# First layers of a fused attention and two-MLP kernel: conversions dealt out evenly, softmax sums on VectorE, transposes later, separate buffers for sums

## The chip, the cores and the metric

The kernel runs on one NeuronCore of a Trainium2 chip. The metric is the device time of one execution in microseconds (us). Engines are named as in the profile: PE is TensorE (matmul), PEld its weight load, DVE VectorE, ACT ScalarE, POOL GpSimd and SP SyncE, which here only issues DMAs.

## The reference

Three steps follow one another, all in float32.

Attention: q, k, v have 4 batches, 8 heads, 768 positions and 64 features. The positions are cut into chunks of 32. A chunk sees 8 memory keys, 16 positions to its left, its own 32 and 8 to its right, 64 keys in all (fewer at the ends). Scores are scaled by 1/8, a softmax (maximum taken away, exponentials, division by their sum plus 1e-9) weighs v.

```python
x = attn_out.transpose(0, 2, 1, 3).reshape(3072, 512)
h = ((x @ w1) * (x @ w2)) @ w3 @ w_out            # w1, w2: 512x1024; w3: 1024x1024; w_out: 1024x512
y = ((h @ w_a) * (h @ w_b)) @ w_out2              # w_a, w_b: 512x1536; w_out2: 1536x512
```

## The kernel before, in words

**Precision.** Every matmul operand of the layers is split into a high part, rounded to the fp32r type by an ACT copy, and a low part, the difference. A product is then three matmuls (`PASSES`: high by high, high by low, low by high). Weights arrive as pairs of 32-bit words. A weight block is rebuilt from them by two scalings on ACT (`w_scale`, L381 and L382) and two operations on DVE (`w_bits`, L386 and L387), and then split.

**Stages.** (1) w3 @ w_out is multiplied out once (`wps`), beside the first attention units. (2) The first layers for token tiles 0 and 1 (512 tokens each) in plain form: for each of 8 column groups a product with w1 (`psA`) and one with w2 (`psB`), the product of both, and then y = g @ (w3 w_out) (`psY`, L816). (3) The first layers for tiles 2 and 3 (t = 2) and 4 and 5 (t = 4) in pair form: `seven12` computes one column group for two tiles as seven products of six matmuls each (Winograd's form of Strassen's scheme), a *pair step* of 42 matmuls. A half of four pair steps is followed by a y pass of 8 groups of 12 matmuls; there are two halves (h = 0 and 1) for each t. The second y pass adds to what the first stored in DRAM. Beside it, `x_build` makes the seven operands x of the next two tiles: it loads eight pieces from DRAM, forms differences (`minus`) and splits each result (`x_put`: high part on ACT, low part on DVE or POOL). (4) The second layers, also with seven products a step (`seven`), with an output product (`ops`).

**Attention** goes in 16 units of 192 tokens. A unit's stages are put into numbered slots: unit u starts at slot BASE[u], 7 slots after the unit before it from the sixth on. Scores (`sc`, in PSUM) come in slot 0, maximum and exponentials in slots 1 and 2 (`a_max`, 16 calls on ACT at L204, each with its sum), normalisation by POOL in slots 2 and 3 (`a_norm`, L221), transposes (`a_trans`, L232) and their copy (`a_pt`, L238) in slot 5, the products with v (`a_pv`, `xp`) in slot 6, the copy out (`a_x`) in slot 7 for units from the sixth on. `paced` spreads the slots over the steps of the layers, so that tile i has its input in time (`NEED`, `GOAL`). PE runs what is issued in that order.

**Conversion of w_a and w_b** (`c_weights`, generator `cw`): 12 blocks, each turned into seven pieces that are written to DRAM (`wcd`). A block is 12 steps: four rebuild its two halves, eight form sums (`add`, L519), split them (high part L102 on ACT, low part L105 on DVE, tile `co`) and issue the writes on SP. One step is taken at a time: in the plain form where nothing else is left to convert (`between`), and at three places in the pair form (`hook`): two in a pair step, one in each group of a y pass. What is left after t = 4 is issued in one loop (L977) before the second layers.

The weights of each pair step are loaded ahead by DMAs on POOL's queue (`w7_load`, L784). Low parts of g are formed on POOL in `g_split` (L876). A PSUM accumulator that gets further products is read between them: by ACT (`copied`, L862) or by DVE (`onto`, L866); PE cannot go on in that bank before.

Of the kernel before, what the change touches and what calls it, by code (L numbers as in the profile page):

```python
# [13 lines left out]
P = 128  # L14
# [11 lines left out]
ND = 2  # L26
# [20 lines left out]
def tile_attention_moe(  # L47
# [135 lines left out]
    def a_max(u):  # L183
# [12 lines left out]
        nc.vector.tensor_scalar_mul(mx, mx, -SCALE)  # L196
        soft[u] = (sc, t, mx, sm)

    def a_exp(i):
        def stage_of(u):  # L200
            sc, t, mx, sm = soft[u]
            for a in range(2 * i, 2 * i + 2):
                for r in range(2):
                    nc.scalar.activation(  # L204
                        t[:, a, r, :],
                        sc[:, r, a, :],
                        AF.Exp,
                        bias=mx[:, r, a : a + 1],
                        scale=SCALE,
                        accum_out=sm[:, a, r : r + 1],  # L210
                    )

        return stage_of

    def a_norm(e):
        def stage_of(u):
            t, mx, sm = soft[u][1:]
            t, sm = t[:, 4 * e : 4 * e + 4], sm[:, 4 * e : 4 * e + 4]
            nc.vector.tensor_scalar_add(sm, sm, 1e-9)
            nc.vector.reciprocal(sm, sm)  # L220
            nc.gpsimd.tensor_tensor(  # L221
                t, t, sm[:, :, :, None].to_broadcast([GQ, 4, 2, KEYS]), ALU.mult
            )

        return stage_of
# [33 lines left out]
    def a_x(u):  # L259
# [7 lines left out]
        for c0, c1 in zip(cuts, cuts[1:]):  # L267
            ti = c0 // TT
            src = xp[..., c0 - t0 : c1 - t0]
            if ti >= ND:  # L270
                xo = att.tile([P, KD, n], F32, tag="xo", bufs=1, name="xo")[:, :, : c1 - c0]
# [21 lines left out]
    for u in range(NA):  # L293
        t0, t1, t2, t3 = SLOTS.get(u, (6, 7, 8, 9) if u < NX else (5, 5, 6, 7))
        for s, stage_of in (
# [12 lines left out]
            (2 * (u > 0), a_exp(2)),  # L308
            (2 * (u > 0), a_exp(3)),
# [6 lines left out]
    for i in range(NT1):  # L316
        u = -(-TT * (i + 1) // (NE * GQ)) - 1
        NEED.append(BASE[u] + (8 if u >= NX else 10))
# [170 lines left out]
    def c_weights():  # L489
# [3 lines left out]
        def halves(items):  # L493
# [55 lines left out]
    co_in = [(stage, 2)]  # L549
# [96 lines left out]
    def d_weights():  # L646
        for m in range(M1):
# [17 lines left out]
            for i, p, q, op in (  # L665
# [11 lines left out]
                co = stage.tile([P, 2, CH // 2], F32R, tag="co", bufs=2, name="wo7")  # L677
# [15 lines left out]
    GOAL = [NEED[0], NEED[1] + 6, NEED[2 * ND - 1], NEED[-1]]  # L693
# [5 lines left out]
    def between():  # L699
# [35 lines left out]
    def x_tmp():  # L735
        if tps:
            return tps[-1].tile([P, TT], F32, tag="tmp", bufs=12 - 4 * len(tps), name="xb")
        ntmp[1] = (ntmp[1] + 1) % 4
        return tq[ntmp[1]]
# [5 lines left out]
    def x_build(xs, src, t, eng):  # L745
        for k in range(2):
            b11, b21, b12, b22 = (
                y_load(x_tmp(), src, t + j, i + k) for j in range(2) for i in (0, 2)
            )

            def minus(z, x, y):
                nc.vector.tensor_tensor(z, x, y, ALU.subtract)  # L752

            yield
# [5 lines left out]
            x_put(xs[3], k, b11, eng)  # L760
            minus(b12, b22, b12)
            yield
            x_put(xs[4], k, b12, eng)
            minus(b11, b22, b11)
            yield
            x_put(xs[2], k, b11, nc.vector)
            minus(b21, b21, b11)
            yield
            x_put(xs[5], k, b22, eng)
            yield  # L770
            x_put(xs[6], k, b21, eng)
            yield

# [16 lines left out]
    for ti in range(ND):  # L790
        last = ti == ND - 1
        gs = {}
        for m in range(M1):
            gs[m] = g_new(m)
            ab_step(w12s[m], xt[ti], gs[m], between)
            if last:
# [8 lines left out]
                else:  # L805
                    tq = wpool.tile([P, 4, CH], F32, tag="w12", name="tq")
                    tq = [tq[:, i, :] for i in range(4)]
# [71 lines left out]
    def seven12(w, ga, gb, hook):  # L879
# [3 lines left out]
        g_split()  # L883
        product(pb, 1, w, True)
        onto(c11, pb, c11, ALU.add)
        hook(1)
# [6 lines left out]
        hook(4)  # L893
        product(pc, 5, w, False)
        onto(c12, pc, c12, ALU.add)
        hook(5)
# [299 lines left out]
```

## Time and profile before

| | |
|---|---|
| median of 3 runs | 1248.08 us (1241.35 to 1250.42) |
| the profiled execution, its own time | 1247.78 us |
| its span, first to last instruction | 1246.0 us |
| mean granted PE clock | 0.929 of full speed |
| busy share of the span: PE, PEld, DVE, ACT, POOL | 87%, 69%, 43%, 39%, 25% |
| mean DMA traffic | 189 GB/s |

Busy shares are means over stages that differ. The page's slices show PE at nine tenths and more in the last 17 of 40 slices, and at 0 to 9 tenths with a granted clock between 0.5 and 1 in the slices before. A row is read by its stage: which engine PE waits for there, and what that engine had in front.

### The profile page before, as it was taken

The numbers are of one execution on the slowest core, as the hardware profiler recorded it, in microseconds if no ns is written. First come the engines' busy times: TensorE is split into PE (matmuls) and PEld (weight loads), VectorE is DVE, ScalarE is ACT, GpSimd is POOL, SyncE is SP. The second block draws the span as 40 slices with busy tenths as digits, with TensorE's granted clock in tenths as the row PEclk, the third lists the DMA queues.
The fourth block names the chain that finished last, engine by engine and source line by source line (L and its number), as shares of the span: only waits on it lengthen the run. The fifth ranks groups of instructions, "written<-read, shape, count | busy, mean of one in ns | idle before, by whom it ended". The sixth has DMA issues, their size and how long they took to land. (4 is left out here: it accounts for less than half of the span.)

```text
span 1246.0 us, 18964 instructions
## 1 busy us (share of the span) xinstructions
PE 1082.4 (87%) x7346; PEld 855.1 (69%) x7346; DVE 536.7 (43%) x870; ACT 481.0 (39%) x1231; POOL 314.3 (25%) x316
## 2 busy tenths in 40 slices
PE   9999886787788895799940499999999999999998
PEld 4457765575567674688730388888888888888887
DVE  6667644424552334554476643435323234232220
ACT  6768533543444442333234533333222223222220
POOL 0103424422331141332230123231133230232310
PEclk9999987888799998799975699999999999999999
DMA  9865588655468476465768656454243434434310
GB/s 372 254 189 174 153 254 270 208 153 175 177 204 264 160 246 201 171 252 195 251 202 286 243 201 221 172 195 160 93 178 125 171 135 144 152 130 167 143 69 34
DMA packets 99546, 234.99 MB, mean 189 GB/s; under 512 B 10240, under 2 KB 43392, under 8 KB 91520
## 3 DMA queue, kind: packets, MB, share of 16 engines
q1 hardware_dynamic: 84272, 138.31, 33.9%
q0 software_dynamic: 14976, 95.43, 20.7%
q8 instruction: 58, 0.95, 0.3%
q14 instruction: 32, 0.26, 0.1%
q10 hardware_dynamic: 208, 0.04, 0.0%
HBM read 176.07 MB, written 57.67 MB: 188 GB/s over the span
## 5 line engine op out<-in xcount | busy, mean ns | idle before, releaser
L850 PE MATMUL ps<-x,w 128*128 128x512 f32 x2184 | 525.3, 400 | 101.1 <-ACT tmp L862 75.1
L850 PEld LDWEIGHTS ps<-x,w 128*128 128x128 f32 x2184 | 420.5, 193 | 197.2 <-ACT tmp L862 78.1
L1014 DVE TENSOR_TENSOR tmp<-ps,tmp 128x512 f32<-128x512 f32 x108 | 74.6, 691 | 266.4 <-PE ps L850 236.2
L862 ACT ACTIVATE tmp<-ps 128x512 f32<-128x512 f32 x143 | 85.6, 599 | 215.9 <-PE ps L850 193.0
L93 PE MATMUL psY<-g,wo 128*128 128x512 f32 x576 | 143.1, 408 | 10.7 <-DVE tmp L866 10.7
L784 POOL DMA_DIRECT2D w<-wc x72 | 39.7, 553 | 416.4 <-PE ps L850 415.9
L93 PEld LDWEIGHTS psY<-g,wo 128*128 128x128 f32 x576 | 112.4, 197 | 36.8 <-DVE tmp L866 12.4
L93 PE MATMUL ops<-wo,g 128*128 128x512 f32 x504 | 118.6, 389 | 0.0
L93 PEld LDWEIGHTS ops<-wo,g 128*128 128x128 f32 x504 | 94.6, 188 | 19.6
L1020 ACT ACTIVATE g<-tmp 128x512 fp32r<-128x512 f32 x66 | 40.8, 633 | 139.4 <-DVE tmp L1019 139.4
L1021 POOL TENSOR_TENSOR g<-tmp,g 128x512 fp32r<-128x512 f32 x66 | 84.2, 1297 | 20.2 <-ACT g L1020 19.4
L204 ACT ACTIVATE t<-sc,mx 96x64 f32<-96x64 f32 x256 | 75.4, 318 | 35.8 <-DVE mx L196 35.8
L221 POOL TENSOR_TENSOR t<-t,sm 96x512 f32<-96x512 f32 x32 | 39.4, 1232 | 146.0 <-DVE sm L220 130.4
L102 ACT ACTIVATE x<-xb 128x512 fp32r<-128x512 f32 x56 | 34.2, 627 | 93.8 <-DVE xb L752 40.9
L93 PE MATMUL ops<-fo,g 128*128 128x512 f32 x288 | 68.2, 389 | 0.0
L93 PEld LDWEIGHTS ops<-fo,g 128*128 128x128 f32 x288 | 54.1, 188 | 11.2
L93 PE MATMUL wps<-w_f 128*128 128x512 f32 x128 | 60.3, 625 | 0.0
L866 DVE TENSOR_TENSOR tmp<-ps,tmp 128x512 f32<-128x512 f32 x47 | 32.4, 690 | 63.7 <-PE ps L850 51.2
L204 ACT ACTIVATION_READ_ACCUMULATOR t<-sc,mx 96x1 f32 x256 | 54.5, 213 | 0.0
L381 ACT ACTIVATE raw<-raw 128x512 f32<-128x512 f32 (+1 forms) x66 | 49.2, 745 | 12.8 <-DMA raw<-in_w3a 8.1
L93 PE MATMUL psA<-xt,w 128*128 128x512 f32 x192 | 51.5, 417 | 1.9 <-DVE w L417 1.8
L93 PE MATMUL psB<-xt,w 128*128 128x512 f32 x192 | 51.7, 422 | 0.0
(87 smaller groups left out, 1100.1 us busy)
## 6 DMA issues: line engine op xcount, KB each, us to landing
w<-wc POOLq DMA_DIRECT2D x36, 1024.0 KB, 6.6
w<-wc POOLq DMA_DIRECT2D x36, 768.0 KB, 4.7
wc<-co SPq DMA_DIRECT2D x84, 256.0 KB
w<-wd POOLq DMA_DIRECT2D x16, 1024.0 KB, 7.6
w<-wd POOLq DMA_DIRECT2D x16, 768.0 KB, 4.7
raw<-in_wab SPq DMA_DIRECT2D x24, 512.0 KB
v<-in_vw SPq DMA_DIRECT2D x64, 168.0 KB
kraw<-in_kt SPq DMA_DIRECT2D x16, 512.0 KB
```

The costliest lines, as they stand in the source:

```text
L93: nc.tensor.matmul(o, lhsT=l, rhs=r, start=first, stop=last)
L102: nc.scalar.activation(hi, src, AF.Copy)
L204: nc.scalar.activation(t[:, a, r, :], sc[:, r, a, :], AF.Exp, bias=mx[:, r, a : a + 1], scale=SCALE, accum_out=sm[:, a, r : r + 1],)
L221: nc.gpsimd.tensor_tensor(t, t, sm[:, :, :, None].to_broadcast([GQ, 4, 2, KEYS]), ALU.mult)
L381: nc.scalar.activation(h, h, AF.Prelu, scale=2.0**-112, alpha=2.0**32)
L784: nc.gpsimd.dma_start(out=t[:, c0:c1].bitcast(F32), in_=src[:, c0:c1])
L850: nc.tensor.matmul(ps, lhsT=w[:, i, a, k, :], rhs=xs[i][:, b, k, :], start=first and n == 0, stop=n == 5, skip_group_check=not first,)
L862: nc.scalar.activation(z, ps, AF.Copy)
L866: nc.vector.tensor_tensor(z, x, y, op)
L1014: nc.vector.tensor_tensor(z, ps, y, ALU.add)
L1020: nc.scalar.activation(g2[:, 0, :], z, AF.Copy)
L1021: nc.gpsimd.tensor_tensor(g2[:, 1, :], z, g2[:, 0, :].bitcast(F32), ALU.subtract)
```

## The change

1. Conversion: `between` takes no step of `cw` any more. `hook(attn, conv)` counts conversion places and takes steps so that 145 steps are spread over 78 of them; there are three in a pair step and one in each group of a y pass. The low parts of `co` move from DVE to POOL; `co` has four buffers from the start instead of two, and the extra pool `cop` is dropped.
2. Softmax: DVE subtracts the maximum from the scores (two operations, PSUM to SBUF), ACT takes two exponentials in place, DVE sums them (two reductions) in `a_norm`. Before, ACT took 16 exponentials with a bias and a sum each.
3. Slots: transposes, their copy, PV and copy out go from slots 5, 5, 6, 7 (for units 3 to 5 from 6, 7, 8, 9) to 8, 8, 9, 10; `NEED` and `GOAL` follow. `paced` in the pair form counts 40 hooks instead of 24. `xo` shares the buffer of `p2`.
4. `g_split` in a pair step comes after product 4 instead of product 0.
5. `x_build`: the differences get tiles of their own, loads are issued three and five steps ahead of their use, work is spread over more steps, three of them a group instead of two; two of the seven low parts move from POOL to DVE and one from DVE to POOL. Loads for the second y pass's sums are issued three groups ahead instead of two.

```diff
@@ a_max / a_exp / a_norm
-        nc.vector.tensor_scalar_mul(mx, mx, -SCALE)
+        for e in range(NE):
+            h = slice(4 * e, 4 * e + 4)
+            nc.vector.tensor_tensor(
+                t[:, h].rearrange("p a r k -> p r a k"),
+                sc[:, :, h],
+                mx[:, :, h, None].to_broadcast([GQ, 2, 4, KEYS]),
+                ALU.subtract,
+            )
...
-    def a_exp(i):
+    def a_exp(e):
         def stage_of(u):
-            sc, t, mx, sm = soft[u]
-            for a in range(2 * i, 2 * i + 2):
-                for r in range(2):
-                    nc.scalar.activation(
-                        t[:, a, r, :],
-                        sc[:, r, a, :],
-                        AF.Exp,
-                        bias=mx[:, r, a : a + 1],
-                        scale=SCALE,
-                        accum_out=sm[:, a, r : r + 1],
-                    )
+            t = soft[u][1][:, 4 * e : 4 * e + 4]
+            nc.scalar.activation(t, t, AF.Exp, scale=SCALE)
...
+            nc.vector.tensor_reduce(sm, t, axis=mybir.AxisListType.X, op=ALU.add)
             nc.vector.tensor_scalar_add(sm, sm, 1e-9)
@@ a_x
-                xo = att.tile([P, KD, n], F32, tag="xo", bufs=1, name="xo")[:, :, : c1 - c0]
+                xo = att.tile([P, KD, n], F32, tag="p2", bufs=1, name="xo")[:, :, : c1 - c0]
@@ slots
-        t0, t1, t2, t3 = SLOTS.get(u, (6, 7, 8, 9) if u < NX else (5, 5, 6, 7))
+        t0, t1, t2, t3 = SLOTS.get(u, (8, 8, 9, 10))
...
-            (2 * (u > 0), a_exp(2)),
-            (2 * (u > 0), a_exp(3)),
...
-        NEED.append(BASE[u] + (8 if u >= NX else 10))
+        NEED.append(BASE[u] + (11 if u > 2 else 10))
...
-    GOAL = [NEED[0], NEED[1] + 6, NEED[2 * ND - 1], NEED[-1]]
+    GOAL = [NEED[0], NEED[1] + 9, NEED[2 * ND - 1], NEED[-1]]
@@ halves
-                    split_lo(lo, x.pop(i - 1), hi)
+                    y = x.pop(i - 1)
+                    nc.gpsimd.tensor_tensor(lo, y, hi.bitcast(F32), ALU.subtract)
...
-    co_in = [(stage, 2)]
+    co_in = [(stage, 4)]
@@ d_weights
-                co = stage.tile([P, 2, CH // 2], F32R, tag="co", bufs=2, name="wo7")
+                co = stage.tile([P, 2, CH // 2], F32R, tag="co", bufs=4, name="wo7")
@@ between
-        else:
-            next(cw, None)
         if ti == ND - 1 and b > NY:
-            for _ in range(2):
+            for _ in range(3):
                 next(xg, None)
@@ x_build
+        nxt = loads(0)
+        yield
+        yield
+        yield
         for k in range(2):
...
-            x_put(xs[1], k, b21, nc.vector)
-            minus(b11, b12, b11)
...
+            b11, b21, b12, b22 = nxt
+            t1 = minus(x_tmp(), b12, b11)
             x_put(xs[0], k, b11, nc.vector)
             yield
+            t2 = minus(x_tmp(), b22, t1)
+            x_put(xs[1], k, b21, eng)
             yield
+            t3 = minus(b12, b22, b12)
+            x_put(xs[2], k, t2, nc.vector)
             yield
+            x_put(xs[4], k, t3, eng)
+            t4 = minus(x_tmp(), b21, t2)
             yield
             x_put(xs[5], k, b22, eng)
+            if k == 0:
+                nxt = loads(1)
             yield
+            x_put(xs[3], k, t1, nc.vector)
             yield
+            x_put(xs[6], k, t4, nc.vector)
+            yield
+            if k == 0:
+                yield
+                yield
@@ seven12
         c11 = copied(pa)
-        g_split()
         product(pb, 1, w, True)
         onto(c11, pb, c11, ALU.add)
-        hook(1)
+        hook(1, 0)
...
         onto(c22, pa, c22, ALU.add)
-        hook(4)
+        g_split()
+        hook(1, 1)
         product(pc, 5, w, False)
         onto(c12, pc, c12, ALU.add)
-        hook(5)
+        hook(0, 1)
         product(pa, 6, w, False)
...
-    def hook(j):
-        if j != 1 and acount[0] < GOAL[-1]:
-            nhook[0] += 1
-            paced(ND, nhook[0], 24)
-        if j != 4:
+        hook(1, 1)
+
+    ncw = [0, 0]
+    NCW = 1 + 12 * M2
+
+    def hook(attn, conv):
+        for _ in range(attn):
+            if acount[0] < GOAL[-1]:
+                nhook[0] += 1
+                paced(ND, nhook[0], 40)
+        ncw[0] += conv
+        while ncw[1] * 78 < ncw[0] * NCW:
+            ncw[1] += 1
             next(cw, None)
@@ y pass
+            y_old(2)
...
-                y_old(j + 2)
-                hook(0)
+                y_old(j + 3)
+                hook(2, 1)
                 if h == 1:
-                    next(xg, None)
-                    next(xg, None)
+                    for _ in range(2 + (j > 0)):
+                        next(xg, None)
```

## Rows read from the trace of the kernel before

**Rows 1.** Stages: length; busy PE, PEld, DVE, ACT, POOL (count); clock, DMA share, GB/s.

```profile
82.05:297.84 215.79, 180.58 (x2273) 144.94 (x2273) 109.02 (x185) 107.71 (x392) 74.36 (x68) 0.90 0.65 198
297.84:326.01 28.17, 17.07 (x55) 12.31 (x53) 13.85 (x23) 13.17 (x40) 9.17 (x8) 0.70 0.56 195
326.01:458.63 132.62, 113.26 (x1282) 91.03 (x1283) 56.33 (x97) 61.03 (x218) 38.10 (x38) 0.94 0.61 204
458.63:545.26 86.63, 67.79 (x265) 53.73 (x264) 43.80 (x62) 26.13 (x50) 26.50 (x24) 0.86 0.60 208
545.26:605.10 59.84, 59.84 (x265) 49.55 (x264) 27.47 (x42) 21.64 (x43) 15.33 (x16) 1.00 0.61 220
605.10:703.90 98.80, 29.06 (x110) 22.16 (x108) 60.48 (x118) 40.81 (x85) 14.73 (x12) 0.66 0.74 252
703.90:1246.00 542.10, 538.22 (x2364) 444.55 (x2364) 176.79 (x272) 151.67 (x255) 129.68 (x140) 1.00 0.40 148
```

**Rows 2.** Timeline of PE: start and duration in us, what ran, matmuls counted.

```profile
85.78 1.19 PE L93 MATMUL sc<-kw,q 64*32 64x64 f32 x96
100.65 0.82 PE L232 MATMUL pt<-id_sb,t 96*128 96x96 f32 x8
169.10 1.60 PE L93 MATMUL xp<-p,v 64*64 64x32 f32 x96
...
567.02 38.24 PE L850 MATMUL ps<-x,w 128*128 128x512 f32 x168
```

**Rows 3.** PE's waits, 84 to 296 us: us in total, times, longest us.

```profile
PE pt L232 <- POOL t L221: 22.7, 9, 5.0
PE xp L93 <- ACT p L238: 5.4, 4, 2.0
PE sc L93 <- issue: 5.2, 2, 4.0
PE psA L93 <- DVE w L417: 1.8, 2, 1.2
```

**Rows 4.** PE's waits, 642 to 704 us.

```profile
PE ps L850 <- ACT tmp L862: 60.8, 1, 60.8
```

**Rows 5.** Busy DVE time of line 519 alone, in a stretch of the stages' table.

```profile
642.00:704.00 62.00, 10.62 (x24) 0.53 0.74 257
```

**Rows 6.** Timeline of all engines, two successive weight blocks of the last conversions.

```profile
665.85 0.65 ACT L381 ACTIVATE raw<-raw 128x512 f32<-128x512 f32 x1
...
666.54 0.43 DVE L386 TENSOR_SCALAR dec<-raw 128x512 uint32<-128x512 uint32 x1
...
667.10 0.69 DVE L387 CUSTOM_DVE_ANT_0 dec<-raw,dec 128x1024 uint16<-128x1024 uint16 x1
...
676.30 0.66 ACT L381 ACTIVATE raw<-raw 128x512 f32<-128x512 f32 x1
```

**Rows 7.** Groups by line, whole span: busy us, mean ns, idle before, releasers.

```profile
L866 DVE TENSOR_TENSOR tmp<-ps,tmp 128x512 f32<-128x512 f32 x47 | 32.4, 690 | 63.7 <-PE ps L850 51.2 <-ACT tmp L862 11.0 <-ACT g L102 1.5
...
L680 POOL TENSOR_TENSOR wo<-ws,wo 128x256 fp32r<-128x256 f32 x32 | 27.0, 850 | 56.5 <-ACT wo L102 48.4 <-DMA v<-in_vw 8.0
...
L204 ACT ACTIVATE t<-sc,mx 96x64 f32<-96x64 f32 x256 | 75.4, 318 | 35.8 <-DVE mx L196 35.8
```

**Rows 8.** Timeline, a rebuilding on DVE beside two subtractions on POOL.

```profile
330.08 2.69 POOL L876 TENSOR_TENSOR g<-tmp,g 128x512 fp32r<-128x512 f32 x2 [1.80 <-ACT g L102]
330.12 1.52 DVE L386 TENSOR_SCALAR dec<-raw 128x512 uint32<-128x512 uint32 x1
...
331.67 1.65 DVE L387 CUSTOM_DVE_ANT_0 dec<-raw,dec 128x1024 uint16<-128x1024 uint16 x1
```

**Rows 9.** PE's waits, 326 to 470 us.

```profile
PE ps L850 <- ACT tq L862: 8.2, 4, 3.5
PE pt L232 <- POOL t L221: 4.0, 3, 2.1
PE ps L850 <- ACT tmp L862: 4.0, 1, 4.0
```

More of the change, by code (lines that the diff above doesn't have):

```diff
@@ L736, in x_tmp @@
         if tps:
-            return tps[-1].tile([P, TT], F32, tag="tmp", bufs=12 - 4 * len(tps), name="xb")
-        ntmp[1] = (ntmp[1] + 1) % 4
-        return tq[ntmp[1]]
+            return tps[-1].tile([P, TT], F32, tag="tmp", bufs=9 - len(tps), name="xb")
+        ntmp[1] = (ntmp[1] + 1) % len(xq)
+        return xq[ntmp[1]]
     def y_load(y, src, t, n):
@@ L745, in x_build, with loads, minus @@
     def x_build(xs, src, t, eng):
-        for k in range(2):
[L747 to L754, printed above, removed]
+        def loads(k):
+            return [y_load(x_tmp(), src, t + j, i + k) for j in range(2) for i in (0, 2)]
+        def minus(z, x, y):
+            nc.vector.tensor_tensor(z, x, y, ALU.subtract)
+            return z
+        nxt = loads(0)
+        yield
+        yield
+        yield
+        for k in range(2):
+            b11, b21, b12, b22 = nxt
+            t1 = minus(x_tmp(), b12, b11)
             x_put(xs[0], k, b11, nc.vector)
             yield
-            x_put(xs[1], k, b21, nc.vector)
-            minus(b11, b12, b11)
+            t2 = minus(x_tmp(), b22, t1)
+            x_put(xs[1], k, b21, eng)
             yield
-            x_put(xs[3], k, b11, eng)
-            minus(b12, b22, b12)
+            t3 = minus(b12, b22, b12)
+            x_put(xs[2], k, t2, nc.vector)
             yield
[L763 to L767, printed above, removed]
+            x_put(xs[4], k, t3, eng)
+            t4 = minus(x_tmp(), b21, t2)
             yield
             x_put(xs[5], k, b22, eng)
+            if k == 0:
+                nxt = loads(1)
             yield
-            x_put(xs[6], k, b21, eng)
+            x_put(xs[3], k, t1, nc.vector)
             yield
+            x_put(xs[6], k, t4, nc.vector)
[3 more added lines that the diff above has]
+                yield
     w7 = []
@@ L806, in tile_attention_moe @@
                     tq = wpool.tile([P, 4, CH], F32, tag="w12", name="tq")
-                    tq = [tq[:, i, :] for i in range(4)]
+                    xq = tq = [tq[:, i, :] for i in range(4)]
+                    for _ in range(3):
+                        x = stage.tile([P, CH, 2], U32, tag="raw64", bufs=3, name="xq")
+                        x = x.rearrange("p c w -> p (c w)").bitcast(F32)
+                        xq = xq + [x[:, :CH], x[:, CH:]]
                     xg = x_build(xs, xd, ND, nc.gpsimd)
@@ L924, in tile_attention_moe @@
                     costack = ExitStack()
-                    cop = costack.enter_context(tc.tile_pool(name="cop", bufs=4, side="right"))
-                    co_in[0] = cop, 4
                     tps.append(tp)
-                    tps.append(costack.enter_context(tc.tile_pool(name="xb", bufs=4, side="right")))
+                    tps.append(costack.enter_context(tc.tile_pool(name="xb", bufs=7, side="right")))
                 xn = [x_new() for _ in range(8)]
```

## The prediction

> **What bounds the kernel now.** I read the stages first, cutting the span where TensorE's work changes [rows 1]. From 703.90 us on TensorE is busy 538.2 of 542.1 us at granted clock 1.00: the second layers leave nothing to win, and of the diff only the order of building x, under their output products, falls there. Everything before loses time. To see how much, I price TensorE's own work at its undisturbed rate: 168 matmuls in 38.24 us are 0.2276 us each; a unit's scores take 1.19 us, its transposes 0.82, its PV products 1.60 [rows 2].
>
> - **Plain form of the first layers** (82.05 to 297.84). 2273 matmuls are 576 of the layers (131.1 us), 9 units' scores (10.7) and 8 units' transposes and PV (19.4): 161 us. The stage takes 215.8 [rows 1]: 55 are lost.
> - **Pair form** (297.84 to 632.53) with what follows up to 703.90. The entry, 54 matmuls: 12.3 of 28.2 us, 15.9 lost. Pair steps and first y pass of t = 2, 378 matmuls with four units' scores and five units' transposes and PV: 102.9 of 132.6, 29.7 lost. Second y pass of t = 2 and entry to t = 4: 264 matmuls are 60.1 of 86.6, 26.5 lost. The rest of t = 4, 264 matmuls again: 60.1 of 59.8, none lost. Second y pass of t = 4 and the first 12 matmuls of the second layers: 24.6 of 98.8, 74.2 lost.
>
> All losses are 201 us: the floor of this order of work is 1045. Next I read who holds TensorE. In the plain form the transposes wait 22.7 us for POOL's normalisation, PV waits 5.4 for the copy of the transposed weights, scores 5.2 for nothing that the profile shows, psA 1.8: 35 us [rows 3]. The other 20 of the 55 pass with TensorE below its rate (granted clock 0.90 [rows 1]): a wait costs some 0.55 of itself again. At the end of the pair form it is one wait of 60.8 us for ScalarE [rows 4]: what is left of the conversion of w_a and w_b is issued in one piece ahead of the second layers. It is 24 of 48 sums [rows 5], six of the twelve blocks, each 10.45 us long (from one block's first scaling to the next's [rows 6]). VectorE, ScalarE and GpSimd are far from full there [rows 1]: it is a chain of latencies.
>
> **The change part by part.** The sum is made against the profiled execution: span 1246.0, time 1247.78, so 1.8 lie around the span; the median of the runs, 1248.08, is 0.3 above it.
>
> *Dealing out the conversions.* The generator has 1 + 12 x 12 = 145 steps. The new hooks count 3 per pair step (16) and 1 per y group (32): 80, of which 78 suffice. So nothing is left to drain, and the entry to the second layers becomes one like that of t = 4. The price moves into the pair form: it holds at most six blocks now (the other six are drained [rows 5]), then all twelve. A block alone is two rebuilt halves (0.43 + 0.69 each) and four half-wide sums (put at the same 0.43) on VectorE: 4 us; four scalings of 0.65 and seven half-wide roundings (at most that each) on ScalarE: 7.2 at most [rows 6]. Six or seven more blocks are up to 28 and 50 us, added to 141 us of VectorE and 122 of ScalarE in the 307 us up to 605.10 (the pieces of [rows 1]): both stay under 60%. What can hurt is the place. Before product 0 of a pair step VectorE must have added product 5 of the step before; between the new hook and that deadline lie two products, 2.7 us, less the add's 0.69 [rows 7]. The hook follows the moved `g_split`, whose two POOL subtractions take 2.69 us together, and beside two such, one rebuilding took 1.52 + 1.65 us [rows 8] against 0.43 + 0.69 alone. A hook carries 145/78 = 1.9 steps, so about 0.3 of the hooks hold a rebuilding, some 1 to 2 us late each; sums, and roundings that wait for them ahead of a PSUM copy, add to it on ScalarE. Bounds per pair step: nothing (t = 4 now ran 264 matmuls without loss, at two steps of conversion per pair step) and 3.2 us (a contended rebuilding in each). I take 1.5, near the middle because it becomes 5.6 steps per pair step: 24 us over 16.
>
> *Low parts from VectorE to POOL.* 84 subtractions, at 0.85 us by the nearest row of the same shape on POOL [rows 7]: 71 us, on top of 89 up to 605.10 [rows 1]: about half full. VectorE is relieved of them. The DMA that writes a block is queued on SP behind POOL's result, and loads of y and x behind that. Four `co` buffers in place of two, and y loads issued three groups ahead, cover one g_split's 2.69 us; uncovered, ScalarE would stop at a later rounding for want of a buffer and TensorE at its next copy (inside the 0 to 3.2).
>
> The stretched rebuilding [rows 8] is the row for what POOL does to VectorE. The Trainium skill ("SBUF — State Buffer", Who interferes with whom) says that an operation of VectorE with two SBUF inputs, or in a 2-port mode, and one of GpSimd that reads SBUF take a lock for their whole length, the other fully blocked. The trace agrees nearly: blocked until each POOL subtraction ends, the two would end at 331.85 and 333.46 us; they ended at 331.64 and 333.32. By this rule POOL's 71 us speak against the change, since each could stop VectorE for as long; by the rows' own sum it is the 24 above.
>
> *Softmax.* Per unit ScalarE loses 16 exponentials of 0.318 us [rows 7], 5.1 in a row, and gets two of 512 columns, put at the scaling's 0.65 [rows 6]. VectorE gets two subtractions from PSUM and two sums, put at 0.69 each [rows 7], for one small multiply: at most 2.8 us a unit, 25 in the plain form on 109 of 216 busy; four PSUM banks hide it there. Without that cover it is rival 2. In the pair form TensorE waits 12.2 us for copies by ScalarE, up to 4.0 at once [rows 9], where the 16 stand ahead of a copy; I take 11 of it, with its clock, as gone (bounds 0 and 12.2 x 1.55 = 19).
>
> *Transposes three slots later.* In the plain form 33 slots go to 22 layer steps of 2.7 us (12 matmuls), so the normalised weights get some 5 us more, and 3.8 from ScalarE; the longest wait for POOL is 5.0 [rows 3]. The 22.7 go, with 12.5 of slow matmuls. PV still comes in the slot after, so its wait stays, as do the scores' and psA's (12.4, with clock 19), and I add 5 for VectorE's longer chain: the loss goes from 55 to 24, **-31** (bounds 0 and -36). In the pair form 4.0 of waits [rows 9] go by the same rule: -6. `xo` in `p2`'s buffer costs nothing: the next `p2` comes five slots on, behind that DMA.
>
> *Building x in buffers of its own, earlier.* For t = 2 nineteen steps fit into the last seven intervals of the plain form at three each, with no conversion beside them: of the entry's 15.9 us I leave 3. At the two later entries VectorE has sixteen operations of 0.69, eight y adds and 15 steps of conversion, some 22 to 27 us in a y pass of 21.8. So VectorE is late there now and after; without the second wait for loads I take 12 of the 26.5, at both entries (bounds 5 and 26.5).
>
> Sum: plain form -31; entry -13; t = 2 middle -11 - 6 + 12 = -5; later entry -14.5; t = 4 middle +12; last entry with the drain 74.2 to 12, -62. Together -114 (rounded once): span 1132, **time 1134 us**, own range 1105 to 1155.
>
> **The rivals.**
> 1. *POOL holds VectorE, and that lands on TensorE.* 48 of 80 hooks lie in pair steps: 43 of the 71 us, on top of my 24: **1177**. For it: [rows 8]. Against: few deadlines in a step, and the adds from PSUM keep 0.69 on average [rows 7]. 18%. The skill's rule above, taken to the end, is this case.
> 2. *The plain form gains nothing.* VectorE stands in the normalisation's chain with four more operations, and PV's wait takes over: 1134 + 31 = **1165**. 12%.
> 3. *All hides.* 19 lost in the plain form, 36 after it, for 24 and 64: **1101**. For it: the undisturbed 264 matmuls. 16%.
> 4. *Slower: the drain is only spread.* Each block holds TensorE as long as in the drain, 10.45 us, plus POOL's stretch, 7 x (0.85 - 0.43) and 2 x 2.05 for the rebuildings: 17.5 x 12 = 210 us for my 24: **1320**. From 11.5 us a block on it eats the whole gain. For it: ScalarE and VectorE run in order, and each copy stands behind conversions. Against: blocks pass in the pair form now, at two steps per pair step, and t = 4 shows none of it. 4%.
> 5. *The dealing leaves the drain*: 1134 + 62 = **1196**. The count of steps speaks against it: 2%.
>
> **How the numbers follow.** The forecast keeps 48%. The range 1090 to 1185 holds it, rival 2 and most of 1 and 3; outside are 4, 5 and tails, some 15%. The runs shown spread over 0.7%, so a measurement tells about 1% from no change. Only rival 4 is not faster: faster 0.95, same 0.02, slower 0.03.
>
> **What would show it.** No TensorE wait over 10 us ahead of the second layers; those starting near 590 us, not 704, and still 542 long. A plain form of about 185 us, its transposes waiting under 3 us in all for POOL. In the pair form, single waits of 1 to 2 us behind VectorE's adds or ScalarE's copies, 20 to 30 us over 16 steps, and rebuildings of 1.5 us where POOL works. Wrong would be: waits of 2 us and more in each pair step, a plain form over 205 us, or second layers that lose time.

## The result and the profile after

The changed kernel takes 1183.48 us in the median of 4 runs (1180.43 to 1186.16), against 1249.25 (1241.35 to 1250.62) of the kernel before on the same chip: a ratio of 0.9485, 95% interval 0.9439 to 0.9532. The forecast was 1134 us: faster as foretold, but with 65 us of gain in place of 114. The time lies 1.5 us inside the upper end of the stated range (1090 to 1185) and above the forecast's own range (1105 to 1155). The profiled execution took 1183.12 us, its span is 1181.3 and its mean granted clock 0.952 (0.929 before).

First the stages of the kernel after from the plain form on, cut where those of [rows 1] are cut and with the same columns (length; busy PE, PEld, DVE, ACT, POOL; clock, DMA share, GB/s).

```profile
79.49:263.73 184.24, 170.27 (x2273) 139.18 (x2273) 136.65 (x209) 78.47 (x147) 80.48 (x70) 0.95 0.73 220
263.73:285.23 21.50, 16.85 (x55) 12.27 (x53) 12.78 (x15) 6.99 (x13) 8.87 (x9) 0.76 0.46 157
285.23:424.22 138.99, 115.11 (x1282) 92.48 (x1283) 69.03 (x114) 58.09 (x112) 55.64 (x65) 0.90 0.75 254
424.22:520.25 96.03, 74.53 (x265) 57.02 (x264) 50.31 (x69) 34.24 (x69) 42.26 (x44) 0.84 0.72 242
520.25:589.99 69.74, 62.95 (x266) 50.32 (x265) 29.31 (x46) 30.75 (x63) 31.80 (x39) 0.98 0.76 264
589.99:638.54 48.55, 30.79 (x109) 21.83 (x107) 23.09 (x32) 14.59 (x29) 20.72 (x21) 0.80 0.68 217
638.54:1181.30 542.76, 537.14 (x2364) 443.71 (x2364) 178.21 (x275) 151.22 (x255) 130.69 (x141) 1.00 0.41 147
```

The plain form is 31.6 us shorter (215.8 to 184.2), the drain is gone (98.8 to 48.6 with the last y pass), the second layers are as they were. But from 285.23 to 589.99 the kernel is slower than before: 139.0 for 132.6, 96.0 for 86.6, 69.7 for 59.8.

TensorE's waits say who holds it (us in total, times, longest). Plain form after, 79 to 263 us:

```profile
PE xp L93 <- ACT p L237: 12.2, 4, 6.2
```

Beside [rows 3], the 22.7 us for POOL's normalisation are gone, the wait of PV for ScalarE's copy has grown from 5.4. The pair form, 263 to 640 us, in place of [rows 4, 9]:

```profile
PE ps L859 <- ACT tmp L871: 22.9, 9, 6.1
PE psY L93 <- DVE tmp L875: 17.4, 4, 8.7
PE ps L859 <- ACT tq L871: 10.2, 3, 5.5
PE psY L93 <- POOL g L885: 5.9, 7, 1.7
```

The one wait of 60.8 is gone, and many smaller ones stand in its place: with the smaller lines 74.4 us in all. Nearly all of it (71.2 us) is behind copies, sums and splits that are late, so the next question is what ScalarE, VectorE and SP were doing. Their waits in the same stretch:

```profile
ACT co L102 <- DVE cs L517: 48.1, 23, 4.9
ACT co L102 <- DMA wc<-co: 22.0, 14, 3.9
...
DVE tmp L875 <- DMA tmp<-yd: 24.6, 2, 12.8
DVE cs L517 <- POOL co L499: 22.8, 13, 2.6
```

The waits of the conversion on ScalarE before, 297 to 605 us:

```profile
ACT co L102 <- DMA wc<-co: 15.1, 5, 5.7
...
ACT co L102 <- DVE cs L519: 0.7, 1, 0.7
```

ScalarE stands 70 us ahead of an item of the conversion that is not ready, for 16 before. VectorE stands 23 us for one of the two `cs` buffers that POOL has not read yet, and 24.6 for loads of y, behind which TensorE stands 2.9 and 1.4. SP stands 131.4 us ahead of the write of a block (L500, waiting for POOL's low part), but it stood there before, too (98.7 us from 297 to 605 us), so this number alone says little. Whatever is queued behind such an item waits too, as one place in the timeline after shows (start, length, what; in brackets the idle time before and its releaser):

```profile
361.64 5.43 SPq L272 DMA_DIRECT2D xd<-xo  x2
361.77 0.74 POOL L499 TENSOR_TENSOR co<-cs,co 128x256 fp32r<-128x256 f32 x1
...
365.93 0.60 ACT L271 ACTIVATE xo<-xp 128x512 f32<-128x512 f32 x1 [6.92 <-DMA xd<-xo]
...
367.16 1.07 SPq L500 DMA_DIRECT2D wc<-co  x2
...
371.61 0.42 ACT L102 ACTIVATE co<-dec 128x256 fp32r<-128x256 f32 x1 [3.68 <-DMA wc<-co]
...
373.49 0.59 ACT L871 ACTIVATE tmp<-ps 128x512 f32<-128x512 f32 x1
...
374.13 3.35 PE L859 MATMUL ps<-x,w 128*128 128x512 f32 x7 [6.09 <-ACT tmp L871]
```

Read it from below. TensorE stood 6.09 us for the copy at 373.49. That copy was behind the rounding at 371.61, which had waited 3.68 us for a `co` buffer, that is for a write to DRAM to end: by its semaphore the first of the two issued from 367.16 on. The low part of that piece had been ready since 362.5 (POOL, 361.77). SP issued the write only at 367.16 because the second write of attention's copy-out stood ahead of it, and that one waited for ScalarE's copy at 365.93, which in turn had waited 6.92 us for the first such write to end, since `xo` has one buffer. So this stall begins in attention's copy-out, and the conversion's buffer carries it to TensorE. The busy shares do not show this: in this stage ScalarE is busy for 58.1 of 139.0 us.

### The profile page after: what moved, and what is told of

Read it like the earlier page. It is cut to its first block, busy times and chain, and to the rows that moved or that the text cites. A ratio compares the mean times of both kernels' runs of the same rounds, so it can differ in the third digit from the quotient of the medians.

```text
span 1181.3 us, 18527 instructions
## 1 busy us (share of the span) xinstructions
PE 1082.9 (92%) x7346; PEld 853.3 (72%) x7346; DVE 556.3 (47%) x840; ACT 423.2 (36%) x751; POOL 377.4 (32%) x394
## 3 DMA queue, kind: packets, MB, share of 16 engines
q0 software_dynamic: 14976, 95.43, 22.5%
## 4 chain that ended last, share of the span: by engine, by line
PE 51%; DMA 7%; issue 4%; POOL 3%; ACT 1%; DVE 1%; SPq 0%; POOLq 0%; ACTq 0%; DVEq 0%
PE ps L859 33%; PE ops L93 17%; DMA wc<-co 2%; POOL co L499 2%; PE psY L93 1%; DMA tmp<-yd 1%; DMA xb<-xd 1%; DMA xd<-xo 1%; POOL g L885 1%; DMA xb<-yd 1%; DMA raw<-in_wab 0%; POOL x L729 0%; DMA raw<-in_w2o 0%; DVE xb L746 0%; DVE tmp L875 0%
## 5 line engine op out<-in xcount | busy, mean ns | idle before, releaser
L859 PE MATMUL ps<-x,w 128*128 128x512 f32 x2184 | 532.3, 403 | 48.8 <-ACT tmp L871 24.6
L93 PE MATMUL psY<-g,wo 128*128 128x512 f32 x576 | 146.3, 412 | 27.4 <-DVE tmp L875 17.4
L220 POOL TENSOR_TENSOR t<-t,sm 96x512 f32<-96x512 f32 x32 | 42.3, 1322 | 109.5 <-DVE sm L219 96.5
L93 PE MATMUL psA<-xt,w 128*128 128x512 f32 x192 | 48.8, 402 | 1.8 <-DVE w L414 1.4
L93 PE MATMUL psB<-xt,w 128*128 128x512 f32 x192 | 49.0, 406 | 0.0
L379 ACT ACTIVATE raw<-raw 128x512 uint32<-128x512 uint32 (+1 forms) x66 | 48.6, 737 | 0.0
L499 POOL TENSOR_TENSOR co<-cs,co 128x256 fp32r<-128x256 f32 x48 | 38.5, 816 | 27.6 <-ACT co L102 21.7
```

Of the source, the lines that this page charges most:

```text
L93: nc.tensor.matmul(o, lhsT=l, rhs=r, start=first, stop=last)
L220: nc.gpsimd.tensor_tensor(t, t, sm[:, :, :, None].to_broadcast([GQ, 4, 2, KEYS]), ALU.mult)
L379: nc.scalar.activation(l, l, AF.Copy, scale=2.0**-29)
L499: nc.gpsimd.tensor_tensor(lo, y, hi.bitcast(F32), ALU.subtract)
L859: nc.tensor.matmul(ps, lhsT=w[:, i, a, k, :], rhs=xs[i][:, b, k, :], start=first and n == 0, stop=n == 5, skip_group_check=not first,)
```

## The experiments

Beside each of them the kernel before ran on the same chip (1246.5 to 1249.4 us in the median), and the ratios are to that. Gains given in us are differences of medians that may come from different chips, so some 3 us in them mean nothing. The first eight take the change apart, the last four follow what those showed.

**Attention's part alone**: the kernel before with softmax, slots, `NEED`, `GOAL` and `xo` of after.

```diff
-        nc.vector.tensor_scalar_mul(mx, mx, -SCALE)
...
+            nc.scalar.activation(t, t, AF.Exp, scale=SCALE)
...
+            nc.vector.tensor_reduce(sm, t, axis=mybir.AxisListType.X, op=ALU.add)
...
-        t0, t1, t2, t3 = SLOTS.get(u, (6, 7, 8, 9) if u < NX else (5, 5, 6, 7))
+        t0, t1, t2, t3 = SLOTS.get(u, (8, 8, 9, 10))
```

> The kernel before with the softmax, slot and goal edits alone; conversions, g_split and x_build as before. If the parts add up as the prediction priced them (plain form -31, pair form of t = 2 about -17 with no denser conversion to pay for it), about 1202 us against 1249, the drain of 60 us still there. If the plain form owes its gain to the conversion steps that left it, or the longer chain of the maximum costs as much as it gains: 1235 to 1250.

Measured: 1217.15 us (1212.45 to 1223.19), ratio 0.976 (0.9717 to 0.9804). Its plain form lasts 199.45 us. TensorE's waits, there and, in the second line, over the whole span, where the drain is:

```profile
PE xp L93 <- ACT p L237: 23.8, 5, 8.1
...
PE ps L847 <- ACT tmp L859: 71.1, 4, 60.5
```

The transposes wait for POOL no more, but PV waits 23.8 us for the copy instead of 5.4: the wait has moved by one step of the unit's chain. 16 us are won in the plain form, not 31; the other 13 lie behind it, where 17 were forecast. The drain's 60.5 us are untouched, as they should be.

**The rest without attention**: the kernel after with the old softmax and slots.

```diff
+        nc.vector.tensor_scalar_mul(mx, mx, -SCALE)
...
-            nc.scalar.activation(t, t, AF.Exp, scale=SCALE)
...
-            nc.vector.tensor_reduce(sm, t, axis=mybir.AxisListType.X, op=ALU.add)
...
-        t0, t1, t2, t3 = SLOTS.get(u, (8, 8, 9, 10))
+        t0, t1, t2, t3 = SLOTS.get(u, (6, 7, 8, 9) if u < NX else (5, 5, 6, 7))
```

> The changed kernel with softmax, slots and goals as before (only the copy of x still shares its buffer). If attention's gain is the plain form's 31 us and a little in t = 2: 1183 + 31 to 45 = 1214 to 1228, with transposes waiting 20 us for POOL again. If the later slots hurt the pair form (attention ends later, and the loads for the second y pass behind it): 1195 to 1205.

Measured: 1203.89 us (1202.07 to 1208.48), ratio 0.9656 (0.9629 to 0.9682). Its plain form lasts 193.34 us; TensorE's longest wait there:

```profile
PE pt L232 <- POOL t L221: 12.2, 6, 3.8
```

So attention's edits are worth 20 us in the kernel after (1203.9 less 1183.5) and 29 in the kernel before, not the 48 that I summed. And the plain form gains 22.5 us without them: its wait for POOL is 12.2, not 22.7. Which of the remaining edits does that (no step of `cw` there, four `co` buffers, x built in its own tiles) was not taken apart.

**Low parts of `co` back on VectorE**: one line of after undone.

```diff
-                    nc.gpsimd.tensor_tensor(lo, y, hi.bitcast(F32), ALU.subtract)
+                    split_lo(lo, y, hi)
```

> The changed kernel with the 84 low parts of the conversions back on DVE. Queue theory: the two buffers of the sums come free sooner, ACT no longer stands 48 us behind DVE's sums nor SP 131 us behind POOL, so TensorE's waits for ACT copies fall by half and the time to about 1168. Port theory: the same direction, but through shorter DVE operations (mean of the rebuilding and of the sums back near 0.69 and 0.42 us) and fewer waits for DVE, time 1150 to 1165. Density theory (DVE too full in the pair form): 36 us more on DVE make it slower, 1190 to 1200.

Measured: 1172.14 us (1169.44 to 1174.61), ratio 0.9395 (0.937 to 0.942): 11 us faster than after. This edit of the change costs time. What it does to the engines is in the groups by line (busy us, mean ns, idle before, releasers), of after:

```profile
L384 DVE CUSTOM_DVE_ANT_0 dec<-raw,dec 128x1024 uint16<-128x1024 uint16 x52 | 42.1, 810 | 6.4 <-DVE dec L383 0.5 <-ACT raw L379 0.2
...
L499 POOL TENSOR_TENSOR co<-dec,co 128x256 fp32r<-128x256 f32 x36 | 31.3, 874 | 35.7 <-ACT co L102 27.2 <-DMA raw<-in_wab 8.3
...
L383 DVE TENSOR_SCALAR dec<-raw 128x512 uint32<-128x512 uint32 x52 | 27.2, 523 | 23.6 <-ACT raw L378 22.6
...
L517 DVE TENSOR_TENSOR cs<-dec 128x256 f32<-128x256 f32 x24 | 13.1, 544 | 11.6 <-POOL co L499 11.0
```

and of this kernel:

```profile
L384 DVE CUSTOM_DVE_ANT_0 dec<-raw,dec 128x1024 uint16<-128x1024 uint16 x52 | 41.8, 804 | 6.1
L383 DVE TENSOR_SCALAR dec<-raw 128x512 uint32<-128x512 uint32 x52 | 25.4, 489 | 17.5 <-ACT raw L378 16.3
L105 DVE TENSOR_TENSOR co<-cs,co 128x256 fp32r<-128x256 f32 x48 | 22.9, 483 | 10.4 <-ACT co L102 10.4
...
L517 DVE TENSOR_TENSOR cs<-dec 128x256 f32<-128x256 f32 x24 | 14.1, 588 | 0.7
```

The rebuildings are hardly longer beside POOL's low parts (810 for 804 ns, 523 for 489). What changes is the last column: VectorE's sums no longer wait for POOL to give a `cs` buffer back (11.0 us in this group, 22.8 in all), and VectorE's low part takes 0.48 to 0.53 us, not 0.82 to 0.87. I expected TensorE's waits for ScalarE's copies to fall by half; those for `tmp` and `tq` fall from 33.1 to 30.9 us. The wait that falls most is that for `g_split`, which stands behind the low parts in POOL's queue:

```profile
PE psY L93 <- POOL g L885: 1.7, 4, 0.6
```

All waits of the pair form are 68.9 us for 74.4, so the rest of the gain is not traced to one cause.

**Loads of x for the next tiles one group earlier**, ahead of the second y pass's first group.

```diff
+            if h == 1:
+                next(xg)
...
-                    for _ in range(2 + (j > 0)):
+                    for _ in range(1 + 2 * (j > 0)):
```

> The changed kernel with the first four loads of x issued right after the first three loads of y, ahead of the second y pass's first matmul instead of behind its first group. Queue theory: DVE no longer stands 6.4 us behind these loads with the y adds behind it; TensorE's waits for the y adds (4.4 and 8.7 us) go, some 12 us: about 1171. Density theory: DVE is full there anyway and the wait comes back a group later: 1180 to 1184.

Measured: 1174.86 us (1171.53 to 1181.61), ratio 0.9424 (0.9388 to 0.946). In the pair form PE's wait for VectorE's y adds falls from 17.4 to 8.6 us. The timeline of after shows where they came from:

```profile
605.12 2.35 SPq L738 DMA_DIRECT2D xb<-yd  x4
...
614.04 1.77 DVE L746 TENSOR_TENSOR xb<-xb 128x512 f32<-128x512 f32 x1 [6.41 <-DMA xb<-yd]
...
618.73 1.65 PE L93 MATMUL psY<-g,wo 128*128 128x512 f32 x3 [8.68 <-DVE tmp L875]
```

VectorE waited 6.41 us for the loads of x and had a y add behind it, for which TensorE waited 8.68.

**Four buffers for the sums instead of two, three for `co` instead of four.**

```diff
-            z = stage.tile([P, CH // 2], F32, tag="cs", bufs=2, name="cs")
+            z = stage.tile([P, CH // 2], F32, tag="cs", bufs=4, name="cs")
...
-    co_in = [(stage, 4)]
+    co_in = [(stage, 3)]
```

> The changed kernel with four buffers for the sums of the conversions instead of two, paid for with three co buffers instead of four. If POOL's hold on the two sums is what stops DVE (22.8 us in the pair form) and ACT behind it: 1172 to 1178. If it is the co buffers and their DMAs (ACT waits 22 us for those already): slower, 1188 to 1195. If neither, 1183.

Measured: 1197.62 us (1196.76 to 1203.19), ratio 0.9609 (0.9581 to 0.9638), 14 us slower than after. ScalarE's waits, 263 to 640 us:

```profile
ACT co L102 <- DMA wc<-co: 61.5, 30, 7.6
...
ACT co L102 <- DVE cs L517: 13.7, 11, 3.0
```

The wait for sums falls from 48.1 to 13.7 us, and that for a `co` buffer rises from 22.0 to 61.5. With sums at hand, it is the writes to DRAM, and the `co` buffers they hold, that the chain waits for. As `co` lost a buffer in the same edit, this does not tell what four buffers for the sums would bring alone. Of the 14 us, 7 lie in the plain form (191.3 us long for 184.2), where the pieces of w1 and w2 go through the same buffers.

**First loads of w_a and w_b earlier**: the generator's first step right after the plain form's last x.

```diff
+    next(cw)
...
-    ncw = [0, 0]
+    ncw = [0, 1]
```

> The changed kernel with the first two raw weight loads issued right after x of t = 2 is built, ahead of the first pair step, instead of one step before their first use. ACT stands 8.3 us behind them and TensorE 5.5 us behind ACT. Queue theory: both go, with the slow matmuls after: 1173 to 1177. If ACT then stands as long behind the next late item: 1181 to 1184.

Measured: 1176.08 us (1172.0 to 1179.45), ratio 0.9426 (0.9393 to 0.9459). TensorE's wait for `tq` in the pair form falls from 10.2 to 3.5 us. The place in the timeline of after:

```profile
287.40 0.65 ACT L378 ACTIVATE raw<-raw 128x512 f32<-128x512 f32 x1 [8.30 <-DMA raw<-in_wab]
...
290.75 1.65 PE L859 MATMUL ps<-x,w 128*128 128x512 f32 x3 [5.53 <-ACT tq L871]
```

**These three edits together** (low parts on VectorE, both earlier loads).

```diff
+                    split_lo(lo, y, hi)
...
+    next(cw)
...
+            if h == 1:
+                next(xg)
```

> The changed kernel with low parts on DVE, x loads early and first weight loads early. If they act on different waits the gains add: 1183 - 11 - 9 - 8 = 1155. If they share the same waits: 1163 to 1170.

Measured: 1151.06 us (1148.97 to 1153.44), ratio 0.9227 (0.9203 to 0.9251). The single gains, 11.3, 8.6 and 7.4, sum to 27; together they are 32. The interval of either earlier load overlaps that of after; that of the three together is far below it.

**No conversion work**: leaves out the arithmetic of `c_weights` and the loads of w_a and w_b; the 84 writes stay, from a constant tile.

```diff
-            for _ in range(4):
-                next(conv)
...
+                nc.sync.dma_start(
+                    out=wcd[f][:, i, :].rearrange("p (l c) -> p l c", l=2), in_=fixed.bitcast(F32)
+                )
```

> The changed kernel without the arithmetic and the raw loads of w_a and w_b: the 84 pieces are written from one constant tile at the same steps (so the second layers multiply by constants). It prices the dealing itself. By the prediction's 1.5 us per pair step plus the late first loads: 1183 - 24 - 8 = 1151. If the dealing costs more, in y passes and entries too: 1125 to 1142. If the loss sits in loads, x and attention instead: over 1165.

Measured: 1103.54 us (1100.24 to 1104.61), ratio 0.8837 (0.8813 to 0.8861). Conversion costs the kernel after 80 us. Its plain form takes 185.8 us, 184.2 in after. The stages behind the entry, cut by the same matmuls:

```profile
285.60:390.10 104.50, 103.87 (x1284) 85.31 (x1283) 44.26 (x74) 36.52 (x61) 33.56 (x34) 1.00 0.86 291
390.10:465.46 75.36, 65.28 (x265) 52.16 (x264) 33.48 (x44) 19.57 (x34) 24.15 (x22) 0.93 0.77 268
465.46:525.30 59.84, 59.84 (x265) 49.55 (x264) 13.46 (x20) 16.29 (x28) 14.59 (x16) 1.00 0.73 263
525.30:558.81 33.51, 28.38 (x110) 21.76 (x108) 18.03 (x24) 9.88 (x17) 11.55 (x10) 0.90 0.76 258
```

All 80 us lie in the pair form: the middle of t = 2 takes 104.5 us for 139.0 of after, the stage with the second y pass of t = 2 75.4 for 96.0, the rest of t = 4 59.8 for 69.7, the last one 33.5 for 48.6; the entry is the same (21.0 for 21.5). The middle of t = 2, with four units of attention in it, runs at granted clock 1.00, the full 2.4 GHz, and all but without loss.

**Roundings on POOL**: after with both earlier loads, and the high parts of `co` made by POOL in place of ScalarE, so that ScalarE has nothing of a block but its scalings.

```diff
-                    split_hi(hi, x[i])
+                    nc.gpsimd.tensor_copy(hi, x[i])
```

> The changed kernel with x loads and first weight loads early, and with the high parts of the conversions formed on POOL too, in front of the low parts there: ACT takes no step of a conversion any more that waits for a buffer, a DMA or a sum (it keeps the scalings). Queue theory: TensorE's waits for ACT's copies (some 20 us in the kernel with three edits) go, and 1183 - 9 - 8 - 20 = 1146 or less, though low parts stay on POOL. If POOL becomes too full (134 us of conversions on it, g_split behind them, TensorE's y pass behind that) or its port holds DVE: 1160 to 1180.

Measured: 1137.36 us (1136.5 to 1142.18), ratio 0.9118 (0.9089 to 0.9146). The new groups on POOL, and TensorE's waits of 263 to 640 us:

```profile
L510 POOL CAST co<-cs 128x256 fp32r<-128x256 f32 x48 | 23.0, 479 | 24.4 <-DVE cs L517 21.4 <-DMA wc<-co 3.0
L510 POOL CAST co<-dec 128x256 fp32r<-128x256 f32 x36 | 19.4, 540 | 23.5 <-DVE dec L384 14.9 <-DMA wc<-co 8.6
...
PE psY L93 <- POOL g L886: 14.5, 4, 4.0
PE ps L860 <- ACT tmp L872: 9.6, 6, 2.5
```

VectorE's wait for the `cs` buffers there:

```profile
DVE cs L517 <- POOL co L499: 28.1, 19, 3.4
```

The two earlier loads, if their single gains add, give 1167.5; the roundings are worth some 30 us more. The waits for VectorE's sums, for its rebuilt halves and for `co` buffers are now in POOL's queue (21.4, 14.9 and 11.6 us), where few deadlines stand behind them, and TensorE's waits for `tmp` fall from 22.9 to 9.6. What is late next is `g_split`, which does stand behind them: 14.5. That wait of VectorE's (28.1 for 22.8) and SP's ahead of the write (137.7 for 131.4) are no shorter than in the kernel after, and yet this kernel is 46 us faster: of the queues of ScalarE, VectorE and SP it is ScalarE's that this run shows to cost. The edit also takes one hand-over between engines out of each piece, which was not tested apart.

**The three together with `g_split` back after product 0.**

```diff
         c11 = copied(pa)
+        g_split()
```

> The kernel with the three edits (low parts on DVE, x loads and first weight loads early) with g_split back behind product 0. The prediction priced the dealing by a rebuilding on DVE that runs beside g_split after product 4; were that the cost, it falls by 10 us and more, to 1140. Queue theory: which POOL work stands beside a rebuilding hardly matters: 1148 to 1155; and ACT has its two roundings ahead of the copy after product 2, which could cost some us: up to 1160.

Measured: 1142.94 us (1140.09 to 1146.52), ratio 0.9151 (0.9125 to 0.9177): 8 us less than the three together. The move of `g_split` behind product 4, for which I had no price, costs in that order of work. VectorE is busy for 571.1 us where it was 582.9 in the three together, for the same 924 instructions, so part of its work seems to have run longer beside `g_split`; the time lies between the 1140 expected if that were the cost and the 1148 to 1155 if it hardly mattered.

**Roundings on POOL and `g_split` after product 0.**

```diff
-                    split_hi(hi, x[i])
+                    nc.gpsimd.tensor_copy(hi, x[i])
...
         c11 = copied(pa)
+        g_split()
```

> The kernel with high and low parts of the conversions on POOL and both early loads, with g_split back behind product 0. In the kernel with low parts on DVE this move gave 8 us. If it was POOL's g_split beside DVE's rebuilding, it gives as much here: 1127 to 1132. If it was ACT's two roundings leaving the crowded end of the pair step, ACT has room here and little is left to win: 1134 to 1140.

Measured: 1130.27 us (1128.58 to 1132.15), ratio 0.9073 (0.9043 to 0.9102). 7 us less than without the second edit, though the two intervals overlap. The time falls in the range expected for POOL's `g_split` beside VectorE's rebuilding (1127 to 1132), but the cause does not follow from it: VectorE is busy for 556.2 us here and 558.8 without the edit, and the rebuilding takes 831 and 828 ns.

**That, with PV one slot later** and the last `g_split` of a half ahead of its last conversion steps.

```diff
-        t0, t1, t2, t3 = SLOTS.get(u, (8, 8, 9, 10))
+        t0, t1, t2, t3 = SLOTS.get(u, (8, 8, 10, 11))
...
+        nsev[0] += 1
+        if nsev[0] % HM == 0:
+            g_split()
```

> The same, with PV and the copy out one slot later (so that the copy of the transposed weights has a step of the layers to itself) and with the last g_split of a half ahead of the last conversion steps. TensorE waits 14.5 us for that copy and 14.5 us for the last g_split. Both gone, with the slow matmuls after them, less what comes back in the entry of t = 2, whose x ends a slot later: 1105 to 1118. If the late end of attention costs what PV gains: 1122 to 1135.

Measured: 1126.98 us (1123.04 to 1127.97), ratio 0.9036 (0.9009 to 0.9063), above the 1105 to 1118 that I expected; the interval overlaps that of the version before it. TensorE's wait in the plain form, and one of the pair form:

```profile
PE xp L93 <- ACT p L237: 11.8, 4, 5.2
...
PE psY L93 <- POOL g L886: 3.3, 6, 1.5
```

The `g_split` edit did its work (11.5 to 3.3 us). The slot did not: PV waits 11.8 us where it waited 14.8. The longest of these waits, 5.24 us, ends with the copy at 183.88:

```profile
178.04 0.42 ACT L102 ACTIVATE wo<-ws 128x256 fp32r<-128x256 f32 x1 [5.89 <-DMA wd<-wo]
...
181.12 0.42 ACT L102 ACTIVATE wo<-ws 128x256 fp32r<-128x256 f32 x1 [2.66 <-DMA wd<-wo]
...
183.88 0.80 ACT L237 ACTIVATE p<-pt 128x768 f32<-128x768 f32 x1
```

ScalarE stood twice ahead of roundings for the pieces of w1 and w2 (`wo`), which are converted beside the plain form and wait for a write to DRAM as those of w_a and w_b do later. So at this place it is ScalarE's queue and not the length of attention's chain that makes the copy late. This is the fastest version found, 56 us below the kernel after.

## Why the prediction was right and wrong

That the time lies in the stated range is partly luck: the pair form lost 115 us where 64 were forecast, and the range reached so far up to hold a rival whose cause the runs do not show. The losses of each stage, priced as in the prediction at undisturbed TensorE work, and the sums (L519 before, L517 after, four to a block) that tell how much conversion lies in it:

| stage | before | forecast | of it for dealing | after | no conversion | sums before, after |
|---|---|---|---|---|---|---|
| plain form | 55 | 24 | 0 | 23 | 25 | 4, 0 |
| entry to t = 2 | 16 | 3 | 0 | 9 | 9 | 0, 0 |
| middle of t = 2 | 30 | 25 | 12 | 36 | 2 | 8, 19 |
| second y pass of t = 2, entry to t = 4 | 26 | 12 | 0 | 36 | 15 | 5, 13 |
| rest of t = 4 | 0 | 12 | 12 | 10 | 0 | 7, 13 |
| last y pass and entry, drain before | 74 | 12 | 0 | 24 | 9 | 24, 4 |
| sum | 201 | 88 | 24 | 138 | 59 | |

The forecast's span of 1132 plus the 50 us of the table, less 2.6 us of the start stage, which I had not foreseen to shorten, plus 0.7 of the second layers is 1180; the span is 1181.3.

- **The drain: right.** No TensorE wait over 8.7 us is left there. The second layers start at 638.5, not near 590, and take the same 542.8.
- **The plain form: right in size, wrong in cause.** 184.2 us for 185, and no transposes waiting for POOL. I gave all of it to softmax and slots. Alone they bring 16 us, and the rest without them 22.5; both together 31.6.
- **Dealing out the conversions: this step failed.** I took 1.5 us in each of 16 pair steps, 24 us. Without this term the forecast loses 40 us in the pair form, and the kernel without conversion loses 34: the rest of the sum holds as a whole, though stage by stage its 3, 13, 12, 0 and 12 stand against 9, 2, 15, 0 and 9, so errors offset each other. With conversion it is 115, with waits of up to 8.7 us where I expected 1 to 2: the term measures 80, some of it for the five blocks that passed there before, too. The table shows where. In the rest of t = 4 the price was right: 10 us for thirteen sums, where 12 were forecast. The stage ahead of it has the same thirteen sums and costs 21 us more with them, the last stage 15 for four sums: there x is built. The middle of t = 2 costs 34 for nineteen sums, where 12 were forecast: there softmax and the copies of attention stand in the same queues, as at 365.93. That x and attention are the reason in these stages was not tested apart. The step put its 1.5 us between nothing, read in the one stage in which the conversion has the queues to itself, and 3.2 for a rebuilding stretched by POOL; even 3.2 makes 51 us over 16 pair steps, so the bound failed with the price. It asked whether the engines were full (they are not) and charged the pair steps alone. What it left out are the items' waits for a sum, a buffer or a write with a copy queued behind: 70 us on ScalarE, for 16 before. Taking the roundings out of that queue brought some 30 us, while the waits of VectorE for `cs` and of SP for the low parts and roundings stayed as long.
- **A row that said less than I took from it** was the 264 matmuls of t = 4 that ran without loss before [rows 1], my lower bound. The sums' own line, in that stage before, and in the same stage after:

```profile
545.26:605.10 59.84, 6.15 (x7) 1.00 0.61 220
```

```profile
520.25:589.99 69.74, 7.59 (x13) 0.98 0.76 264
```

Seven sums are under two blocks, thirteen over three, and their low parts have moved from VectorE to POOL. One dense stage without loss said nothing of a denser one.

- **Low parts to POOL at nothing: failed, by 11 us.** I named the buffers as cover; I had not counted `cs`, of which there are two and for which VectorE waits 22.8 us, nor that `g_split` stands behind the low parts in POOL's queue. Of TensorE's waits it is that for `g_split` that falls with them gone, from 5.9 to 1.7 us; that the wait for `cs` is the price is not shown, for with the roundings on POOL it is 28.1 in a faster kernel.
- **Building x "without the second wait for loads": failed.** VectorE still waits 6.4 us for them, and a y add stands behind it: the four loads are issued on SP at 605.12 and used from 612.6 on. Loading earlier brings 9 us.
- **Entry to t = 2:** 3 us forecast, 9 measured, and 9 without conversion work: VectorE's part of the split of x is late by itself, at the moment TensorE needs it. This was priced too low, and it has nothing to do with the dealing.
- **A wait costs 0.55 of itself again: held.** 74.4 us of waits in the pair form go with 115 us of loss, 1.54 to 1. With the same floor it is 1.46 to 1.70 in the eleven other versions that hold the new order of conversion.

The rivals. *POOL holds VectorE* named the time nearest to the result, 1177, but not its cause: the rebuildings are shorter on average than before (810 and 523 ns for 868 and 582), and taking the low parts off POOL shortens them by 6 and 34 ns, 2 us in all 52. A single rebuilding does get stretched [rows 8], and there the Trainium skill ("SBUF — State Buffer", Who interferes with whom) agrees in having the two engines block each other for an operation's whole length. Whether TensorE pays for that over the whole of the work stays open. Putting `g_split` back behind product 0 took 8 us off the three together, and 11.8 off VectorE's busy time; with the roundings on POOL it took 7, and 2.6. Low parts on POOL cost 11 us, not the 43 of this rival. *The plain form gains nothing* named a wait that does take over: PV's, 23.8 us with attention's edits alone, 12.2 with the rest. *All hides*, 1101, is near what the kernel without conversion takes, 1103.5. *The drain is only spread* had the mechanism, copies behind conversions in engines that run in order; its price was 17.5 us a block and the measured one is 80 / 12 = 6.7, short of the 11.5 from which the gain is lost. The dealing left no drain.

**Open** stays what the 80 us split into. The first load's 7 is measured, and the 30 by which ScalarE is freed of roundings follow if single gains add; the fastest version is still 23 us above the kernel without conversion, and that difference is not assigned to an engine. It understates what conversion still costs, since the kernel without conversion has neither the earlier loads of x nor the moves of `g_split` and PV. One buffer more for `xo`, at which the stall of 374.13 begins, was not tried. Nor was it tried to keep conversion out of the groups of the y passes in which x is built.

## What to carry to other kernels

When work is dealt out into the gaps of another loop, price it by the queue, not by the engine's busy time: for each dealt item ask what it waits for, and which copy or load with a deadline is issued behind it on the same engine. Put the items that wait longest on the engine with the fewest deadlines (here POOL instead of ScalarE, some 30 us), issue loads ahead of them, and follow a stall upstream through every queue and buffer before naming its cause: the one at 374.13 looked like the conversion's and began in attention's copy-out. A price read in a stage where the work has the queues to itself holds for that stage alone.

## What was not expected of the hardware

- A rounding copy of 128x256 to fp32r took POOL 0.48 to 0.54 us, ScalarE 0.41 (412 to 413 ns, 84 of them): POOL is only a sixth or a third slower there, while its subtraction of the same size took 0.82 to 0.87 against VectorE's 0.48 to 0.53.
- POOL at work did not lengthen VectorE's rebuildings on the mean (810 and 523 ns beside 70 us more of POOL work, 868 and 582 before), although a single one beside two long subtractions took two to four times as long [rows 8]. Where POOL works still matters: with `g_split` two products away VectorE's busy time fell from 582.9 to 571.1 us for the same instructions.
